# Merging the first unit's rows earlier, reads that do not hold scatters, plane copies on one engine, and a tile that starts elsewhere

## The chip, the cores and the metric

The kernel runs on one core of a Trainium2 chip, in one launch. The time is the device time of an execution in microseconds (us); the number that counts is the median of several. Engines are named as in the profile: PE is TensorE (PEld its weight loads), DVE is VectorE, ACT is ScalarE, POOL is GpSimd and SP is SyncE. Times of the trace count from the start of the span.

## The reference

Three stages follow one another, all in fp32:

```python
# 1. linear attention: batch 8, heads 8, sequence 576, head size 64
kv  = einsum('bhsd,bhse->bhde', k, v)
out = einsum('bhsd,bhde->bhse', q, kv)
x   = out / sqrt(mean(out*out, -1) + 1e-6) * g_norm      # -> 4608 tokens x 512
# 2. three first products, their maximum and relu, one second product (768 wide)
h = maximum(maximum(maximum(x @ w1, x @ w2), x @ w3), 0)
x = h @ w_out
# 3. 8 experts, the 2 best of each token by noisy logits
noisy = x @ w_gate + log1p(exp(x @ w_noise)) * noise
top2_w = exp(v - max(v)); top2_w /= sum(top2_w) + 1e-9   # v: the two best of noisy
for e in range(8):
    for k in range(2):
        out[mask] += top2_w[mask, k] * (maximum(x[mask] @ W1[e], 0) @ W2[e])   # W1 512x1024
```

## The kernel before

Each operand of a product is kept as a high part and a low part (the rest), both in a form that TensorE reads at full pace, and a product is three matmuls: high by high, weight's high by low, weight's low by high (the list `PASS`).

The program has two halves. **Chunks:** the 4608 tokens are done in nine chunks of 512. For each, `g1` makes the first products of stage 2 (L311), and `window(c)` the second product `g2` (L357) in four blocks of 128 tokens, each in two halves (`g2(c, i, 0, 3)`, `g2(c, i, 3, 6)`). Behind a block's second half its logits are copied out (L360) and its 512 values are cut in two planes of 16 bits and put into the tile RA (L364: half of the copies on VectorE, half on ScalarE). Routing (`route_a`, `route_b`) finds each token's two experts and its place among an expert's rows. `scatter(c, k)` writes the rows, with their weight and token number, to a table Xg in DRAM by four writes of GpSimd (L427), one for each block, for the best (k = 0) and the second expert (k = 1). The scatters of a chunk run in the next one. In chunk 8, at steps 11 to 17, the expert with most rows so far is picked (`spec_pick`) and the first work on it begins: its weights are loaded and split, and `load_rows(0)` reads 512 of its rows.

**Units:** the rows of the experts are done in 25 units of 512, 256 or 128 rows, that is four, two or one blocks. Units 0 to 3 have four, and then units of four alternate with smaller ones: units 4, 6 and 8 have one block, the even ones from 10 on two. Each has eight steps f. G1 (L1059; for one block L1073, rows by weights) makes 128 hidden columns; ScalarE and VectorE make their high and low parts behind relu (L1063, L1064). G2 (L1121) adds the second product, in four banks or fewer, and comes two steps later, by a queue (`fifo`); ScalarE scales its result (L1126) and GpSimd adds it to the output by row number (L1095). In a one-block unit, G1 makes 256 columns at every second f, as rows; two steps later `turn` has them transposed on TensorE (`hT1`, L1084), after ScalarE's relu (L1076), and ScalarE and VectorE make their parts (L1085, L1086).

The rows of a unit come in by `load_rows`: a transposing read on SyncE's queue (L755) of the planes, to RB (unit 0 and odd units) or RA, and a small read of weight and token number (`gt`, L756). `utrans(u, i)` then *merges* block i of unit u: two copies put the planes together as fp32 in one of two tiles mg (L784, the first on VectorE, the second on ScalarE), ScalarE writes the high part (L787), VectorE the low part (L788). The parts of even units go to one pair of tiles, those of odd units to B2 (high) and xlo (low). xlo holds 512 rows for all odd units, since these have four blocks.

Weights are loaded by SyncE as pairs (`load_pair`) and split by `splits`: ScalarE writes the high part (L292), VectorE the low part (L293), in a ring of 12 tiles W. The table `SPL` says how many splits follow each step of a unit.

Instructions are put on each engine's queue in the order in which the code emits them, and an engine takes them in that order. A framework adds the waits: an instruction waits for whatever wrote its inputs or still uses its output tile. For DRAM it can be told that accesses do not depend on each other (`declare_no_dep`, by group); the scatters are in such a group, "xg", and a read of rows gets by hand a dependency on every scatter issued so far (the list `written`). Before the change, a scatter issued after a read of rows waits for that read, since both touch Xg.

The order around the handover from chunks to units is written out: steps 11 to 17 of chunk 8 (`misc1`) with `load_rows(0)` at 12 and chunk 7's second scatter at 14, then `window(8)`. There, `nx` is false, and `trans(i)` means `utrans(0, i)`.

Of the kernel before, what the change touches and what calls it, by code (L numbers as in the profile page):

```python
# [12 lines left out]
U16 = mybir.dt.uint16  # L13
# [72 lines left out]
def body(tc, A, dbg=None):  # L86
    nc = tc.nc
    PE, ACT, DVE, POOL, SP = nc.tensor, nc.scalar, nc.vector, nc.gpsimd, nc.sync
# [8 lines left out]
    def st(name, shape, dt=F):  # L97
        return sb.tile(shape, dt, name=name)

    Xg = dr.tile([XR, 2 * XW], U16, name="Xg")  # L100
# [243 lines left out]
    rows = RA.rearrange("p (i w) -> p i w", i=4)  # L344
# [274 lines left out]
    for s in range(12):  # L619
# [6 lines left out]
        u = 2 + 0.1 * s if s > 1 else (0.2, 0.4)[s]  # L626
# [20 lines left out]
    for g in range(18):  # L647
# [4 lines left out]
        f = g // 3  # L652
# [62 lines left out]
    order = order + spare  # L715
    units = [{"S": 4, "4": 4, "2": 2, "1": 1}[k] for k, _ in order]
    regE, regS = {}, {}
    st("al1", [128, 16])
    spi = st("spi", [128, 3], I32)
    spf = st("spf", [128, 3])  # L720
    sp1 = st("sp1", [128, 8])
# [22 lines left out]
    gt = [st(f"gt{i}", [128, 4, 2]) for i in range(3)]  # L744
# [3 lines left out]
    def rplanes(u):  # L748
        n = 128 * units[u]
        return rbuf(u).bitcast(U16)[:, 0:8 * n].rearrange("p (k t) -> p k t", k=8)  # L750

    def load_rows(u):
        m = units[u]
        at = bass.ds(regS[u], 128 * m)
        for i in (SP.dma_start_transpose(out=rplanes(u), in_=Xg[at, 0:1024]),  # L755
                  SP.dma_start(gt[u % 3][:, 0:m, :].bitcast(U16),  # L756
                               Xg[at, 1024:1028].rearrange("(i p) w -> p i w", p=128))):
            for w in written:
                tc.add_manual_dep(i.ins, w.name, mybir.DependencyInfo(mybir.DependencyClass.Sync,
                                                                      mybir.DependencyReason.DATA), reason="rows")  # L760

    praw = {}

# [10 lines left out]

    xTu = [xT]

    def utrans(u, i):
        s = slice(i * 128, (i + 1) * 128)
        pl = rplanes(u)
        g = MG[mgn[0] % 2]  # L780
        mgn[0] += 1
        h = g.bitcast(U16).rearrange("p (k t z) -> p k t z", k=4, z=2)
        for q in range(2):
            (ACT.copy if q else DVE.tensor_copy)(h[:, :, :, q], pl[:, 4 * q:4 * q + 4, s])  # L784
        t = g.rearrange("p (k t) -> p k t", k=4)
        x = xTu[u % 2]
        ACT.activation(x[0][:, :, s], t, AF.Copy)  # L787
        DVE.tensor_tensor(x[1][:, :, s], t, x[0][:, :, s].bitcast(F), op=OP.subtract)  # L788
        if i == units[u] - 1:
            m = units[u]  # L790
            DVE.tensor_copy(wid[u % 3][:, 0:m], gt[u % 3][:, 0:m, 0])
            DVE.tensor_copy(idt[u % 3][:, 0:m], gt[u % 3][:, 0:m, 1])
# [71 lines left out]
    def window(c):  # L864
        nx = c + 1 < NCH

        def fill(i):
            if nx:
                if i == 0:
                    ao(c + 1, 1, [hbank(), hbank()])  # L870
                norm(c + 1, i + 2)

        def trans(i):
            xtrans(c + 1, i) if nx else utrans(0, i)

        if c == 0:
            for i in (2, 3):
                g2(0, i, 0, 3)
                trans(i)
                g2(0, i, 3, 6)  # L880
            xn_n[0] = 0
            return
        for i in range(4):
            g2(c, i, 0, 3)
            if i == 3:
                trans(2)
                trans(3)
            g2(c, i, 3, 6)
            if i == 1:
                trans(0)  # L890
                trans(1)
                fill(0)
                fill(1)
            if not nx:
                if i == 3:
                    load_rows(1)
                splits(1)

# [133 lines left out]
    fifo = []  # L1032
# [99 lines left out]
    def turn(s):  # L1132
        while late and late[0][0] <= s:
            hT1(*late.pop(0)[1:])

    def flush(s):
        while fifo and fifo[0][0] <= s:
            G2(*fifo.pop(0)[1:])

# [20 lines left out]

    pump = {0: 1, 2: 1, 3: 2, 4: 2, 5: 2, 6: 2, 8: 1, 9: 1}
    tg = table()
    SPL = {4: (2,) * 8, 2: (1,) * 8, 1: (0, 0, 0, 1, 0, 1, 1, 1)}

    def unit(u):
        mn = units[u + 1] if u + 1 < len(units) else 0
        for f in range(8):
            turn(step[0])
            G1(u, f)
            flush(step[0])  # L1170
            for _ in range(pump.get(step[0], 0)):
                next(tg, None)
            if u < 2:
                if f in (3, 5):
                    for i in range(2):
                        utrans(u + 1, f - 3 + i)
                if u == 1 and f == 7:
                    load_rows(3)
            splits(SPL[units[u]][f])
            if u > 1:  # L1180
                if f in (2, 4):
                    for i in range(f - 2, min(f, mn)):
                        utrans(u + 1, i)
                if f == (4 if mn == 4 else 2) and u + 2 < len(units):
                    regs_of(u + 2)
                    load_rows(u + 2)
                    loads()
            step[0] += 1
# [7 lines left out]
    for u in range(NUN):  # L1196
        unit(u)
# [52 lines left out]
```

## Time and profile before

| | |
|---|---|
| time, median of 3 runs | 1570.40 us (1568.75 to 1570.77) |
| time of the profiled execution | 1571.03 us |
| its span | 1569.3 us |
| PE busy | 1523.7 us, 97% |
| DVE busy | 789.9 us, 50% |
| ACT busy | 655.0 us, 42% |
| POOL busy | 219.2 us, 14% |
| G1 of the units (L1059), both operands | 464.8 us in 2112 matmuls |
| G2 of the units (L1121) | 441.5 us in 1800 matmuls |
| chunks' first products (L311) | 456.3 us in 2160 matmuls |

The span is the time between the first and the last instruction of the trace; the profiled execution took 1.7 us more than its span. A group's busy time counts the time in which at least one of its instructions ran. A wait is the time in which an engine stood idle before an instruction, put down to what ended it. Matmuls overlap in the pipeline, so the pace of TensorE is read from start to start, or from the chain of waits, which gives each piece only the time that no other covers.

### The profile page before, as it was taken

To read this page: it belongs to the slowest core of one execution; us is meant where nothing else is said; L and a number is where in the kernel's file an instruction comes from. 1 tells how busy PE (TensorE), PEld (TensorE's weight loads), DVE (VectorE), ACT (ScalarE), POOL (GpSimd) and SP (SyncE) were. 2 spreads that over 40 slices of the span, in tenths; PEclk is the share of its full clock that TensorE was granted. 3 is DMA by queue.
4 is the path that set the end of the run, shared out by engine and by line. 5 is a ranking of instruction groups with operands and counts; after the bars stand their busy time and mean duration, and the time that the engine had idled before them with its cause. 6 is when DMAs were issued, how large, how long until landed. Compare 5 with 4: busy or idle time off the path is not lost.

```text
span 1569.3 us, 23768 instructions
## 1 busy us (share of the span) xinstructions
PE 1523.7 (97%) x9564; PEld 1308.5 (83%) x9564; DVE 789.9 (50%) x1561; ACT 655.0 (42%) x1048; POOL 219.2 (14%) x326
## 2 busy tenths in 40 slices
PE   6999999999999999999999898999999999999997
PEld 5789989898989888887888787778888888888886
DVE  4985534353434343456454456365463554535543
ACT  3544323231313132243454446455464554645544
POOL 0000211102020202023211102101021010211102
PEclk8999999999999999999999999999999999999999
DMA  7322642031212101063676467666695766857654
GB/s 291 134 81 89 257 189 115 29 116 53 91 56 89 56 28 55 1 189 115 209 195 137 112 221 186 158 204 173 159 223 130 199 156 166 210 139 215 148 154 76
DMA packets 132292, 219.82 MB, mean 140 GB/s; under 512 B 96464, under 2 KB 96720, under 8 KB 114640
## 3 DMA queue, kind: packets, MB, share of 16 engines
q1 hardware_dynamic: 112320, 166.50, 33.4%
q0 software_dynamic: 19856, 51.73, 14.6%
q8 instruction: 77, 1.26, 0.3%
q14 instruction: 39, 0.32, 0.1%
HBM read 146.30 MB, written 51.72 MB: 126 GB/s over the span
## 4 chain that ended last, share of the span: by engine, by line
PE 51%; DVE 2%; ACT 2%; issue 0%; POOL 0%; POOLq 0%; ACTq 0%; DVEq 0%
PE bank L1059 25%; PE bank L1121 25%; ACT B L787 1%; PE bank L1073 1%; DVE G L930 0%; ACT W L292 0%; DVE xlo L788 0%; DVE mg L784 0%; DVE W L293 0%; POOL out L1095 0%; PE bank L1084 0%; ACT mg L784 0%; ACT xn L1076 0%; DVE B L1064 0%; DVE h L1086 0%
## 5 line engine op out<-in xcount | busy, mean ns | idle before, releaser
L311 PE MATMUL bank<-B,W 128*128 128x512 f32 (+1 forms) x2160 | 456.3, 372 | 6.4 <-ACT W L482 4.0
L311 PEld LDWEIGHTS bank<-B,W 128*128 128x128 f32 x2160 | 378.0, 190 | 76.0 <-ACT W L482 4.8
L1121 PE MATMUL bank<-W,B 128*128 128x512 f32 x1728 | 421.8, 390 | 0.0
L1121 PEld LDWEIGHTS bank<-W,B 128*128 128x128 f32 x1728 | 320.2, 188 | 65.6
L1059 PE MATMUL bank<-B,W 128*128 128x512 f32 (+1 forms) x1728 | 358.9, 345 | 5.4 <-ACT B L787 5.4
L1059 PEld LDWEIGHTS bank<-B,W 128*128 128x128 f32 x1728 | 281.9, 190 | 51.7 <-ACT B L787 6.0
L293 DVE TENSOR_TENSOR W<-G,W 128x1024 fp32r<-128x1024 f32 x200 | 242.2, 1223 | 123.4 <-ACT W L292 122.6
L292 ACT ACTIVATE W<-G 128x1024 fp32r<-128x1024 f32 x200 | 207.8, 1054 | 54.2 <-PE bank L1121 40.3
L1064 DVE SCALAR_TENSOR_TENSOR B<-bank,B 128x512 fp32r<-128x512 f32 (+1 forms) x176 | 103.7, 591 | 220.7 <-ACT B L1063 220.7
L1063 ACT ACTIVATE B<-bank 128x512 fp32r<-128x512 f32 (+1 forms) x176 | 90.6, 517 | 282.0 <-PE bank L1059 281.8
L357 PE MATMUL bank<-W,B 128*128 128x256 f32 (+1 forms) x1296 | 163.9, 285 | 0.0
L357 PEld LDWEIGHTS bank<-W,B 128*128 128x128 f32 x1296 | 160.1, 188 | 1.1
L427 POOL DMA_INDIRECT Xg<-RA,si x72 | 71.0, 986 | 529.9 <-issue 346.3
L329 DVE TENSOR_TENSOR hm<-hm,bank 128x512 f32<-128x512 f32 (+1 forms) x106 | 69.5, 656 | 132.4 <-PE bank L311 125.6
L315 ACT ACTIVATE B<-hm 128x512 fp32r<-128x512 f32 (+1 forms) x53 | 32.2, 607 | 185.2 <-DVE hm L329 185.2
L1059 PE MATMUL bank<-xlo,W 128*128 128x512 f32 x384 | 105.9, 398 | 0.0
L1095 POOL DMA_INDIRECT out<-xn,idt x37 | 60.8, 1644 | 276.8 <-ACT xn L1126 269.8
L1059 PEld LDWEIGHTS bank<-xlo,W 128*128 128x128 f32 x384 | 72.6, 189 | 16.4
L787 ACT ACTIVATE B<-mg 128x512 fp32r<-128x512 f32 x76 | 48.0, 632 | 71.9 <-DVE mg L784 71.8
L1095 POOL DMA_INDIRECT out<-x2T,idt x19 | 30.2, 1589 | 268.5 <-ACT x2T L1126 266.1
L364 ACT COPY RA<-bank 128x256 uint16<-128x256 uint16 x72 | 25.7, 372 | 89.0 <-DVE RA L364 77.1
L788 DVE TENSOR_TENSOR xlo<-mg,B 128x512 fp32r<-128x512 f32 x49 | 34.0, 693 | 38.7 <-ACT B L787 38.7
(184 smaller groups left out, 1020.1 us busy)
## 6 DMA issues: line engine op xcount, KB each, us to landing
G<-mw SPq DMA_DIRECT2D x100, 1024.0 KB, 5.0
G<-w1s SPq DMA_DIRECT2D x12, 1024.0 KB, 5.1
out<-pad POOLq DMA_DIRECT2D x1, 9472.0 KB
kv<-kv SPq DMA_DIRECT2D x8, 1024.0 KB, 8.2
G<-kv SPq DMA_DIRECT2D x8, 1024.0 KB, 10.1
RB<-qT SPq DMA_DIRECT2D x8, 1024.0 KB, 5.0
G<-kvr SPq DMA_DIRECT2D x7, 256.0 KB, 10.2
Xg<-RA,si POOLq DMA_INDIRECT x72, 2.7
```

Source lines behind the costliest of these rows:

```text
L292: ACT.activation(w[:, 0:1024], src, AF.Copy)
L293: DVE.tensor_tensor(w[:, 1024:2048], src, w[:, 0:1024].bitcast(F), op=OP.subtract)
L311: PE.matmul(bank[:, 0:t1 - t0], w_in(g)[:, a, k, s], x[b][:, k, t0:t1], start=n == 0 and k == 0, stop=n == 2 and k == 3)
L329: DVE.tensor_tensor(hm, hm, bank, op=OP.max)
L357: PE.matmul(x2b[i][z][:, 0:hi - lo], h[:, a, s], w[:, b, lo:hi], start=f == 0 and n == 0, stop=f == 5 and n == 2)
L427: i = POOL.indirect_dma_start(out=Xg, out_offset=bass.IndirectOffsetOnAxis(ap=idx, axis=0), in_=src, in_offset=None)
L787: ACT.activation(x[0][:, :, s], t, AF.Copy)
L1059: PE.matmul(bank[:, 0:n], w[:, a, k, s], x[b][:, k, 0:n], start=z == 0, stop=z == 11)
L1063: ACT.activation(h[:, 0, 0:n], bank[:, 0:n], AF.Relu)
L1064: DVE.scalar_tensor_tensor(h[:, 1, 0:n], bank[:, 0:n], 0.0, h[:, 0, 0:n].bitcast(F), op0=OP.max, op1=OP.subtract)
L1095: d = POOL.indirect_dma_start(out=A["out"], out_offset=bass.IndirectOffsetOnAxis(ap=idt[u % 3][:, i:i + 1], axis=0), in_=y, in_offset=None ...
L1121: PE.matmul(obank[i], h[:, a, s], w[:, b, ff % 2, :], start=ff == 0 and n == 0, stop=ff == 7 and n == 2)
```

## The change

Six edits. (1) A tile of 16 values a partition, `al1`, becomes one of 8, so every tile that is allotted later starts 32 bytes lower: xlo from byte 215328 of a partition (32 past a multiple of 64) to 215296 (a multiple of 64), and the two mg the other way, the first from 209792 to 209760. (2) The reads of rows of units 0 and 1 join the group "xg", so that scatters issued after them do not wait for them. (3) `utrans` gets `tight`: in a one-block unit both plane copies are made by VectorE. (4) In `window(8)`, blocks 0 and 1 of unit 0 are merged behind block 0, blocks 2 and 3 and the read of unit 1's rows behind block 1; before, the first two came behind block 1, the others in the middle of block 3 and the read at its end. (5) The queue `fifo` is sorted by unit and step, and G1 stands before `turn`. (6) `SPL` of one-block units puts fewer splits in the steps before the last two.

```diff
@@ -715,7 +715,7 @@
     order = order + spare
     units = [{"S": 4, "4": 4, "2": 2, "1": 1}[k] for k, _ in order]
     regE, regS = {}, {}
-    st("al1", [128, 16])
+    st("al1", [128, 8])
     spi = st("spi", [128, 3], I32)
     spf = st("spf", [128, 3])
     sp1 = st("sp1", [128, 8])
@@ -752,12 +752,18 @@
     def load_rows(u):
         m = units[u]
         at = bass.ds(regS[u], 128 * m)
-        for i in (SP.dma_start_transpose(out=rplanes(u), in_=Xg[at, 0:1024]),
-                  SP.dma_start(gt[u % 3][:, 0:m, :].bitcast(U16),
-                               Xg[at, 1024:1028].rearrange("(i p) w -> p i w", p=128))):
+        ds = [SP.dma_start_transpose(out=rplanes(u), in_=Xg[at, 0:1024]),
+              SP.dma_start(gt[u % 3][:, 0:m, :].bitcast(U16),
+                           Xg[at, 1024:1028].rearrange("(i p) w -> p i w", p=128))]
+        for i in ds:
+            if u < 2:
+                tc.declare_no_dep(i.ins, group="xg", reason="rows of chunks that came before")
             for w in written:
                 tc.add_manual_dep(i.ins, w.name, mybir.DependencyInfo(mybir.DependencyClass.Sync,
                                                                       mybir.DependencyReason.DATA), reason="rows")
+        if u < 2:
+            for i in ds:
+                tc.add_to_no_dep_group("xg", i.ins)
 
     praw = {}
 
@@ -774,14 +780,14 @@
 
     xTu = [xT]
 
-    def utrans(u, i):
+    def utrans(u, i, tight=False):
         s = slice(i * 128, (i + 1) * 128)
         pl = rplanes(u)
         g = MG[mgn[0] % 2]
         mgn[0] += 1
         h = g.bitcast(U16).rearrange("p (k t z) -> p k t z", k=4, z=2)
         for q in range(2):
-            (ACT.copy if q else DVE.tensor_copy)(h[:, :, :, q], pl[:, 4 * q:4 * q + 4, s])
+            (ACT.copy if q and not tight else DVE.tensor_copy)(h[:, :, :, q], pl[:, 4 * q:4 * q + 4, s])
         t = g.rearrange("p (k t) -> p k t", k=4)
         x = xTu[u % 2]
         ACT.activation(x[0][:, :, s], t, AF.Copy)
@@ -882,17 +888,20 @@
             return
         for i in range(4):
             g2(c, i, 0, 3)
-            if i == 3:
+            if nx and i == 3:
                 trans(2)
                 trans(3)
             g2(c, i, 3, 6)
-            if i == 1:
+            if nx and i == 1:
                 trans(0)
                 trans(1)
                 fill(0)
                 fill(1)
             if not nx:
-                if i == 3:
+                if i < 2:
+                    trans(2 * i)
+                    trans(2 * i + 1)
+                if i == 1:
                     load_rows(1)
                 splits(1)
 
@@ -1134,6 +1143,7 @@
             hT1(*late.pop(0)[1:])
 
     def flush(s):
+        fifo.sort(key=lambda x: x[1:3])
         while fifo and fifo[0][0] <= s:
             G2(*fifo.pop(0)[1:])
 
@@ -1160,13 +1170,13 @@
 
     pump = {0: 1, 2: 1, 3: 2, 4: 2, 5: 2, 6: 2, 8: 1, 9: 1}
     tg = table()
-    SPL = {4: (2,) * 8, 2: (1,) * 8, 1: (0, 0, 0, 1, 0, 1, 1, 1)}
+    SPL = {4: (2,) * 8, 2: (1,) * 8, 1: (0, 0, 0, 0, 0, 0, 1, 1)}
 
     def unit(u):
         mn = units[u + 1] if u + 1 < len(units) else 0
         for f in range(8):
+            G1(u, f)
             turn(step[0])
-            G1(u, f)
             flush(step[0])
             for _ in range(pump.get(step[0], 0)):
                 next(tg, None)
@@ -1180,7 +1190,7 @@
             if u > 1:
                 if f in (2, 4):
                     for i in range(f - 2, min(f, mn)):
-                        utrans(u + 1, i)
+                        utrans(u + 1, i, units[u] == 1)
                 if f == (4 if mn == 4 else 2) and u + 2 < len(units):
                     regs_of(u + 2)
                     load_rows(u + 2)
```

Edit 4 on VectorE, in chunk 8's window from block 0's copies on. B_85 holds the parts of unit 0's rows, mg_280 and mg_281 are the merge buffers, W_75 and W_76 tiles of split weights. Before:

```order
L364 COPY RA<-bank_110 128x256
L364 COPY RA<-bank_111 128x256
L293 TENSOR_TENSOR W_75<-G_84,W_75 128x1024
L360 COPY lgs<-bank_109 128x16
L364 COPY RA<-bank_112 128x256
L364 COPY RA<-bank_109 128x256
L784 COPY mg_280<-RB 128x512
L788 TENSOR_TENSOR B_85<-mg_280,B_85 128x4x128
L784 COPY mg_281<-RB 128x512
L788 TENSOR_TENSOR B_85<-mg_281,B_85 128x4x128
L293 TENSOR_TENSOR W_76<-G_82,W_76 128x1024
```

After:

```order
L364 COPY RA<-bank_110 128x256
L364 COPY RA<-bank_111 128x256
L790 COPY mg_280<-RB 128x512
L794 TENSOR_TENSOR B_85<-mg_280,B_85 128x4x128
L790 COPY mg_281<-RB 128x512
L794 TENSOR_TENSOR B_85<-mg_281,B_85 128x4x128
L293 TENSOR_TENSOR W_75<-G_84,W_75 128x1024
L360 COPY lgs<-bank_109 128x16
L364 COPY RA<-bank_112 128x256
L364 COPY RA<-bank_109 128x256
L790 COPY mg_280<-RB 128x512
```

Four merges move ahead: two past the split of W_75, and two past the splits of W_76 and W_77 and block 2's copies (of the second two the first copy is the last row).

Edit 5 on TensorE, from the first transposes of unit 4 (one block) to G1 of unit 5 (four blocks). xn_93 is the row of hidden values, L1084 the transposes, L1073 its G1, L1059 that of unit 5. Before:

```order
L1084 MATMUL bank_107<-cst,xn_93 128x128 x2
L1073 MATMUL bank_108<-W_72,B_85 128x256 x12
L1084 MATMUL bank_105<-cst,xn_93 128x128 x2
L1073 MATMUL bank_106<-W_74,B_85 128x256 x12
L1121 MATMUL bank_110<-W_71,h_0_6243 128x512 x6
L1084 MATMUL bank_107<-cst,xn_93 128x128 x2
L1073 MATMUL bank_108<-W_76,B_85 128x256 x12
L1121 MATMUL bank_110<-W_73,h_1_6244 128x512 x6
L1084 MATMUL bank_105<-cst,xn_93 128x128 x2
L1059 MATMUL bank_106<-B_87,W_78 128x512 x4
```

After (lines shifted by 9, so that L1093 are the transposes, L1082 and L1068 the two G1):

```order
L1082 MATMUL bank_107<-W_72,B_85 128x256 x12
L1093 MATMUL bank_108<-cst,xn_93 128x128 x2
L1082 MATMUL bank_105<-W_74,B_85 128x256 x12
L1093 MATMUL bank_106<-cst,xn_93 128x128 x2
L1130 MATMUL bank_110<-W_71,h_0_6243 128x512 x6
L1082 MATMUL bank_107<-W_76,B_85 128x256 x12
L1093 MATMUL bank_108<-cst,xn_93 128x128 x2
L1130 MATMUL bank_110<-W_73,h_1_6244 128x512 x6
L1068 MATMUL bank_105<-B_87,W_78 128x512 x4
L1093 MATMUL bank_106<-cst,xn_93 128x128 x2
```

Each transpose moves behind the G1 that followed it, the last one behind the first G1 of unit 5 (of its twelve matmuls the first four are shown).

Edits 3 and 6 on ScalarE, in the same unit. L1076 is relu, L784 a plane copy, L787 the high part, L1085 the high part of the transposed row, L292 a split. Before:

```order
L1085 ACTIVATE h_0_6243<-bank_107 128x256
L1076 ACTIVATE xn_93<-bank_108 128x256
L784 COPY mg_281<-RB 128x512
L787 ACTIVATE B_87<-mg_281 128x4x128
L784 COPY mg_280<-RB 128x512
L787 ACTIVATE B_87<-mg_280 128x4x128
L292 ACTIVATE W_80<-G_84 128x1024
L1085 ACTIVATE h_1_6244<-bank_105 128x256
L1076 ACTIVATE xn_93<-bank_106 128x256
```

After (L1085 is relu here, L1094 the transposed row's high part, L793 the merge's):

```order
L1085 ACTIVATE xn_93<-bank_107 128x256
L1094 ACTIVATE h_0_6243<-bank_108 128x256
L793 ACTIVATE B_87<-mg_281 128x4x128
L793 ACTIVATE B_87<-mg_280 128x4x128
L1085 ACTIVATE xn_93<-bank_105 128x256
L1094 ACTIVATE h_1_6244<-bank_106 128x256
L793 ACTIVATE B_87<-mg_281 128x4x128
L793 ACTIVATE B_87<-mg_280 128x4x128
L1085 ACTIVATE xn_93<-bank_107 128x256
L1094 ACTIVATE h_0_6243<-bank_108 128x256
L292 ACTIVATE W_80<-G_84 128x1024
```

The plane copies are gone, and the split of W_80 moves from between the merges to behind all four.

## Rows read from the trace of the kernel before

**Rows 1.** The page: busy us (share of the span) and instructions.

```profile
PE 1523.7 (97%) x9564; PEld 1308.5 (83%) x9564; DVE 789.9 (50%) x1561; ACT 655.0 (42%) x1048; POOL 219.2 (14%) x326
```

**Rows 2.** Waits of TensorE, whole span: total us, times, longest.

```profile
PE bank L1084 <- ACT xn L1076: 12.2, 9, 2.2
PE bank L1059 <- ACT B L787: 5.4, 2, 5.2
```

**Rows 3.** Timeline, TensorE, chunks to units: start, us, instructions, [idle before <- releaser].

```profile
685.97 17.73 PE L357 MATMUL bank<-W,B 128*128 128x256 f32 x144
708.91 10.19 PE L1059 MATMUL bank<-B,W 128*128 128x512 f32 x36 [5.22 <-ACT B L787]
718.94 2.88 PE L1121 MATMUL bank<-W,B 128*128 128x512 f32 x12
721.67 0.19 PE L412 MATMUL bank<-Cb,onesb 128*128 128x40 bf16 x1
```

**Rows 4.** Stretch 700 to 720: length, busy us of engines, clock, DMA share.

```profile
700.00:720.00 20.00, 14.78 (x72) 12.52 (x71) 10.85 (x40) 10.18 (x18) 0.00 (x0) 0.83 0.26 53
```

**Rows 5.** Timelines of SyncE, VectorE and GpSimd around chunk 7's second scatter.

```profile
673.64 11.45 SPq L755 DMA_TRANSPOSE RB<-Xg  x1
679.89 0.17 DVE L435 COPY RA<-wt 128x4 f32<-128x4 f32 x1
689.25 1.40 POOL L427 DMA_INDIRECT Xg<-RA,si  x1 [18.29 <-DMA gt<-Xg]
```

**Rows 6.** Timelines of VectorE and ScalarE (last row), merges of unit 0.

```profile
692.44 0.76 DVE L364 COPY RA<-bank 128x256 uint16<-128x256 uint16 x2 [1.71 <-DMA Xg<-RA,si]
694.65 1.23 DVE L293 TENSOR_TENSOR W<-G,W 128x1024 fp32r<-128x1024 f32 x1 [1.45 <-ACT W L292]
696.53 0.46 DVE L784 COPY mg<-RB 128x512 uint16<-128x512 uint16 x1
708.89 0.69 DVE L788 TENSOR_TENSOR B<-mg,B 128x512 fp32r<-128x512 f32 x1 [0.76 <-ACT B L787]
708.23 0.63 ACT L787 ACTIVATE B<-mg 128x512 fp32r<-128x512 f32 x1 [0.53 <-DVE mg L784]
```

**Rows 7.** Chain of waits, units 2 and 3: start, us, pieces.

```profile
832.00 2.72 PE bank L1059 x12
834.72 2.72 PE bank L1121 x12
837.44 2.77 PE bank L1059 x12
840.21 2.73 PE bank L1121 x12
```

**Rows 8.** Groups by form, TensorE: count, busy us, mean ns.

```profile
L1059 PE MATMUL bank<-xlo,W 128*128 128x512 f32 x384 | 105.9, 398 | 0.0
```

**Rows 9.** Timeline, TensorE, one-block unit 4 into unit 5.

```profile
895.18 0.44 PE L1084 MATMUL bank<-cst,xn 128*128 128x128 f32 x2 [1.41 <-ACT xn L1076]
900.64 0.69 PE L1084 MATMUL bank<-cst,xn 128*128 128x128 f32 x2 [2.19 <-ACT xn L1076]
900.99 2.06 PE L1059 MATMUL bank<-B,W 128*128 128x512 f32 x4
```

**Rows 10.** Timelines of VectorE, GpSimd and ScalarE in unit 4.

```profile
889.77 0.77 DVE L784 COPY mg<-RB 128x512 uint16<-128x512 uint16 x1
891.10 1.57 POOL L1095 DMA_INDIRECT out<-xn,idt  x1 [0.27 <-issue]
895.02 0.77 ACT L784 COPY mg<-RB 128x512 uint16<-128x512 uint16 x1
```

**Rows 11.** Stretch 900 to 904, columns as in rows 4.

```profile
900.00:904.00 4.00, 3.35 (x10) 2.73 (x11) 3.92 (x5) 2.75 (x6) 0.00 (x0) 0.57 0.41 113
```

**Rows 12.** Timelines of TensorE and ScalarE, start of unit 9.

```profile
1038.24 5.61 PE L1121 MATMUL bank<-W,B 128*128 128x512 f32 x24
1038.88 0.68 ACT L1126 ACTIVATE xn<-bank,wid 128x512 f32<-128x512 f32 x1
```


## The prediction

> **What bounds the kernel now.** I read the page's busy shares first, then what TensorE waited for, then the timelines around those waits, and last the chain of waits for the pace of matmuls that wait for nothing. TensorE is busy for 1523.7 us [rows 1] of a span of 1569.3, so time can be gained only where it waits, where its clock is granted low, or where its matmuls run slower than others of their kind. The table of waits names two places that this change touches: 12.2 us in nine waits of the one-block units' transposes (L1084) for ScalarE's row of hidden values, and 5.4 us in which G1 (L1059) waits for ScalarE's high part of a unit's rows (L787), 5.2 of them at once [rows 2].
>
> The one of 5.2 is the handover from the chunks to the units. Its matmuls end the last product of chunk 8 at 703.70, and G1 of unit 0 starts at 708.91 [rows 3]. It is paid twice, since the granted clock over 700 to 720 is 0.83 [rows 4]: 0.17 of 20 us, doubled, is some 6.8 us at the lower level (1.2 GHz), part of it after the idle time. So the 36 matmuls of three G1 took from 708.91 to 718.94, 10.03 us.
>
> Why the rows were late is in the rows of the other engines. SyncE issued the transposing read of unit 0's rows from 673.64 on. The second scatter of chunk 7 had its last operand from VectorE at about 680.1, but GpSimd started it at 689.25, after an idle 18.29 us that the read of the same rows ended [rows 5]. Until it had read its planes, VectorE could not copy block 0 of chunk 8 into them (692.44, after 1.71 idle), so the split of W (694.65) and the first merge (696.53) queued behind that, and the last high and low parts of unit 0 came at 708.23 and 708.89 [rows 6].
>
> **The change part by part.** *Handover.* The reads of units 0 and 1 no longer hold the scatters. Nothing else in front of them on GpSimd's queue moves, so chunk 7's second scatter starts at about 680.2 instead of 689.25 and its planes are free some 3.2 us later (692.44 less 689.25 is what block 0's copies waited for), at 683.4. Block 0 of chunk 8 is through TensorE at 685.97 plus a quarter of 17.73, 690.4 [rows 3], so its copies now wait only for the product. Block 0's four plane copies end at about 691.4 on VectorE (0.76 for its two [rows 6]). The merges of rows 0 and 1 follow there, each 0.46 (copy), 0.63 (high part), 0.69 (low part) [rows 6] and semaphores, about 2.1 in all for one that is alone, 1.8 when the copies lie beside the other: they end at 695.7. The split of W (1.23) ends at 697.2, block 1's copies at 698.4, and the merges of rows 2 and 3 at 702.2. G1 wants them at 703.7, so the wait of 5.2 goes with 1.5 to spare, and with it the drop of the clock: 10.03 less 3 x 2.72 [rows 7] is 1.87. That is 7.1; I take 7.0. Next late: block 1's copies must free their banks for block 3, which starts at 685.97 + 3 x 4.43 = 699.3 (0.9 to spare), and routing of chunk 8, whose counts TensorE sums at L412. That stood at 721.67 in a row with matmuls on both sides [rows 3] and comes 7 us earlier, while block 3's copies and the chain behind them come only 4 to 5 earlier; I work out 0.2 to 1.0 us to spare. SyncE's read for unit 1 moves up from 708 to 702; nothing stands behind it there that could go sooner. Bounds: 0 (the wait moves whole to a copy or the routing) and 8.5.
>
> *The aligned low part.* The shorter tile shifts all later tiles by 32 bytes, so xlo, at 32 past a multiple of 64 bytes before, starts on such a multiple; the merge buffers go the other way. xlo is the moving operand of the middle four matmuls of a G1 in odd units of two and four blocks. Unit 2, whose low part lies in another tile, shows G1 of 12 matmuls in 2.72 us and G2 in 2.72; unit 3, with xlo, 2.77 and 2.73 [rows 7]. Neither unit waits and the clock is whole. There are 384 such matmuls [rows 8], so 96 groups: 96 x 0.05 = 4.8, and with the 0.01 of the G2 behind, 5.8. I take 5.3. Odd units differ from even ones in nothing else that TensorE reads: same weights' ring, same shapes, and the high parts of both start on a multiple of 64. But no row shows xlo at another place, so the bounds are 0 and 5.8. A cost of merge buffers at 32 bytes: VectorE wrote xlo there in 0.69, as it did the aligned low part of unit 0 (0.69 [rows 6]); I set it to nothing.
>
> *One-block units.* In each of the three that run (units 4, 6, 8) the four-block unit that follows is merged. Twelve copies of 0.77 leave ScalarE [rows 10] and go to VectorE at 0.46, where the low part of the same merge now stands behind two copies in a row. A merge that was two copies side by side, 0.63 and 0.69 becomes 2 x 0.46, 0.63, 0.69, in one line: 2.25 to 2.3 against the 1.82 at which merges followed one another. Four of them and GpSimd's row writes beside the first two (a copy took 0.77 there [rows 10]) bring the last high part to about 900.3. G1 of the next unit now stands ahead of the last transposes on TensorE and waits for that high part instead: it starts at about 900.35, where in the trace of before it started at 900.99, behind its transposes [rows 9]. Of the three waits of a unit, 1.41 and 2.19 [rows 9] and the 0.47 that they leave of a third of 12.2, the first in time (0.47) goes, the second stays at some 1.2 to 1.7, and the third becomes one of about 2.45 at G1. Gain 0.4 a unit, 1.2 in all, with 0 and 1.2 a unit as its ends. Against that stand the splits that move to the end of these units and beyond: 2.0 us more of ScalarE lies in front of the merges in the first steps of the next unit. In unit 9, which merges a two-block unit at its end, ScalarE read the last output bank of unit 8 from 1038.88 to 1039.56; TensorE writes it anew with the tenth matmul after 1038.24, at 1040.3 [rows 12]. That slack of 0.7 is less than 2.0, so 1.3 is lost there, up to 2.0. And the one wait of 2.45 is longer than any before: the clock fell after unit 4's waits alone (0.57 over 900 to 904 [rows 11]), so this can give 1.4 back or cost as much in two more units. Together I take +0.4, between -5 and +5.
>
> Sum: 1571.03 (the profiled execution: span and 1.7 around it) - 7.0 - 5.3 + 0.4 = 1559.1. The median of the runs shown lies 0.63 lower, so 1558.5.
>
> **The rivals.** *The low part's slowness is not its place.* Then 5.3 stays: 1563.8. For it: in unit 3's G1 the four matmuls behind those on xlo are slow too, though they read the aligned high part, and only one place was ever run. Against: unit 2 and every G1 of unit 0 lack it.
>
> *The one-block waits go away*, as two engines share the merges better: 12.2 and the 1.4 of clock, 1558.5 - 14.0 = 1544.5. For it: ScalarE is the releaser of all nine. Against: the chain of copies above, which no engine shortens.
>
> *The rows come too late all the same.* The second scatter's four writes now run beside the transposing read, which took 11.45 us to issue [rows 5]; if they push its landing out by more than the 2 to 4 us to spare, or if the copies of block 1 come late for block 3, the wait of 5.2 stays in another place: 1558.5 + 7.0 = 1565.5. Against: TensorE's table shows no other wait on row reads, and only their sum must fit.
>
> *Slower: copies and row writes shut each other out.* In one-block units VectorE now makes eight copies of planes in a row while GpSimd writes the rows of the unit before, four writes of 1.57 us [rows 10]. If a copy could not run beside a write at all, each unit's merges would come up to 4 x 1.57 = 6.3 us later, straight onto G1: 19 us in three units, 1577. It decides once it costs more than the 11.9 that the other parts gain, 4 us a unit. Against it, one copy of 0.77 instead of 0.46 is all that the rows show of before, 0.31 a copy. The Trainium skill (SBUF — State Buffer, section "Who interferes with whom") has such a rule: a copy in a two-port mode and GpSimd take a shared pair of ports whole, and whoever comes second blocks fully. By that rule the trace agrees only in part: the copy was lengthened, but by a fifth of a write.
>
> **How the numbers follow.** A difference under 0.2%, 3.1 us, can't be told from none here. My forecast has 0.65; the low part unchanged 0.13; the one-block waits gone 0.07; the rows late 0.10; the copies shut out 0.05. Faster by over 0.2% means under 1567.3: all but the last, and but a tail of the late rows joined with an unchanged low part (1570.8): 0.92. Within 0.2% 0.04, slower 0.04. The forecast's own range is 1555 to 1562; reaching to the first and third rival gives 1553 to 1566, which leaves out the one-block waits gone and the copies shut out.
>
> **What would show it.** Handover: no wait of G1 at L1068 (1059 before) above 0.5 after the last product of chunk 8, clock 1.00 there, and GpSimd's scatter at about 680. Low part: unit 3's G1 in 2.72, and the mean of 96 groups down by 0.05. One-block units: a wait of about 2.4 at G1 for L793 in each, and one of 1 to 2 at L1130 at the start of unit 9. Wrong would be a time above 1566 or under 1553, G1 still at 2.77, or a wait at L412 or in the product of chunk 8 that takes up what the handover gives.

## The result and the profile after

The kernel after took 1556.27 us (median of 4, 1555.68 to 1557.19) where the kernel before took 1569.95 (median of 4): a ratio of 0.9914, 95% interval 0.9897 to 0.9931, or 13.7 us. 1558.5 was forecast. The profiled execution has a span of 1554.0 us.

The table of waits of TensorE, whole span, as [rows 2] of before (total us, times, longest):

```profile
PE bank L1068 <- ACT B L793: 6.9, 4, 2.3
PE bank L1130 <- ACT xn L1135: 1.9, 1, 1.9
PE bank L1093 <- ACT xn L1085: 0.8, 3, 0.3
```

The nine waits of 12.2 at the transposes are down to 0.8, and the handover's 5.2 is gone; in their place stand three waits of 2.3 at G1 (their fourth is small), and one of 1.9 at G2. Around the handover (timeline of TensorE, then a window with the granted clock behind POOL's count, then POOL, VectorE and ScalarE), answering [rows 3 to 6]:

```profile
684.57 17.73 PE L357 MATMUL bank<-W,B 128*128 128x256 f32 x144
702.13 8.33 PE L1068 MATMUL bank<-B,W 128*128 128x512 f32 x36
710.30 2.88 PE L1130 MATMUL bank<-W,B 128*128 128x512 f32 x12
```

```profile
700.00:720.00 20.00, 20.00 (x100) 16.77 (x99) 14.44 (x61) 9.38 (x17) 2.93 (x5) 1.00 0.32 78
```

```profile
678.47 1.69 POOL L427 DMA_INDIRECT Xg<-RA,si  x1 [8.93 <-DVE RA L435]
689.24 0.75 DVE L364 COPY RA<-bank 128x256 uint16<-128x256 uint16 x2
689.91 0.46 DVE L790 COPY mg<-RB 128x512 uint16<-128x512 uint16 x1
700.23 0.69 DVE L794 TENSOR_TENSOR B<-mg,B 128x512 fp32r<-128x512 f32 x1 [0.76 <-ACT B L793]
699.56 0.63 ACT L793 ACTIVATE B<-mg 128x512 fp32r<-128x512 f32 x1 [0.51 <-DVE mg L790]
```

The product of chunk 8 ends and G1 follows without a gap; 36 matmuls take 8.2 us to the next row's start (before: 10.03), and the clock of the window is 1.00 (before: 0.83). GpSimd's scatter starts with its operand, block 0's copies (689.24) wait only for the product, and the last high part (699.56 and 0.63) is 1.9 us ahead of G1.

The low part, from the chain of waits in unit 3, where before had 2.77 and 2.73 [rows 7], and the group of its matmuls, 398 ns each before [rows 8]:

```profile
839.14 2.72 PE bank L1068 x12
841.86 2.72 PE bank L1130 x12
```

```profile
L1068 PE MATMUL bank<-xlo,W 128*128 128x512 f32 x384 | 103.2, 391 | 0.0
```

In unit 4, and the same in 6 and 8 (timelines of TensorE, then VectorE and GpSimd; answers to [rows 9, 10]):

```profile
885.05 0.44 PE L1093 MATMUL bank<-cst,xn 128*128 128x128 f32 x2 [0.24 <-ACT xn L1085]
889.30 1.21 PE L1068 MATMUL bank<-B,W 128*128 128x512 f32 x4 [2.26 <-ACT B L793]
```

```profile
881.18 0.79 DVE L790 COPY mg<-RB 128x512 uint16<-128x512 uint16 x2
883.27 0.79 DVE L790 COPY mg<-RB 128x512 uint16<-128x512 uint16 x2
877.64 1.56 POOL L1104 DMA_INDIRECT out<-hm,idt  x1 [32.03 <-ACT hm L1135]
881.38 1.65 POOL L1104 DMA_INDIRECT out<-xn,idt  x1 [0.27 <-issue]
883.34 1.79 POOL L1104 DMA_INDIRECT out<-xn,idt  x1 [0.27 <-issue]
```

The transposes wait 0.24, and G1 of unit 5 waits 2.26 for the last high part. Two copies in a row take 0.79, less than twice 0.46, so a merge follows the other after 2.1 us (881.18 to 883.27). And at unit 9, against [rows 12] (TensorE, then ScalarE; the last row is a window with its clock):

```profile
1027.57 5.30 PE L1130 MATMUL bank<-W,B 128*128 128x512 f32 x15 [1.88 <-ACT xn L1135]
1032.71 1.08 PE L1068 MATMUL bank<-B,W 128*128 128x512 f32 x4
```

```profile
1020.10 2.00 ACT L292 ACTIVATE W<-G 128x1024 fp32r<-128x1024 f32 x2
1022.00 0.77 ACT L790 COPY mg<-RA 128x512 uint16<-128x512 uint16 x1
1026.84 0.68 ACT L1135 ACTIVATE xn<-bank,wid 128x512 f32<-128x512 f32 x1
```

```profile
1027.00:1033.00 6.00, 5.43 (x17) 4.34 (x18) 3.28 (x6) 2.41 (x3) 1.60 (x2) 0.72 1.18 277
```

The split of 2.00 stands ahead of the merges, the scaling of unit 8's rows (1026.84) comes 1.9 us late, and then 15 matmuls take 5.1 us to the next start where 3.4 is their time at the pace of unit 3 (12 in 2.72): the granted clock is 0.72 over six us.

**Where the time went.** The starts of the same matmuls in the two traces, as differences after less before: -1.4 us up to the last product of chunk 8 (-1.5 arises in the first 85 us, which the change doesn't touch, so it is put down to the two executions); -5.4 at G1 of unit 0 and -1.9 more by its first G2 (handover, -7.2); -0.53 in each of twelve odd units (low part, -6.4); units 4 to 9 together +0.1 without their three parts of that; -0.3 at the end. Their sum is -15.3, the difference of the two spans.

### The profile page after: what moved, and what is told of

Read it like the earlier page. It is cut to its first block, busy times and chain, and to the rows that moved or that the text cites. A ratio compares the mean times of both kernels' runs of the same rounds, so it can differ in the third digit from the quotient of the medians.

```text
span 1554.0 us, 23767 instructions
## 1 busy us (share of the span) xinstructions
PE 1515.0 (97%) x9564; PEld 1306.2 (84%) x9564; DVE 792.4 (51%) x1573; ACT 646.0 (42%) x1036; POOL 221.4 (14%) x326
## 4 chain that ended last, share of the span: by engine, by line
PE 92%; DVE 3%; ACT 2%; DMA 1%; issue 1%; POOL 1%; SPq 0%; POOLq 0%; ACTq 0%
PE bank L311 28%; PE bank L1068 24%; PE bank L1130 24%; PE bank L357 10%; PE bank L192 1%; PE bank L214 1%; PE bank L273 1%; DVE mg L790 1%; ACT B L793 1%; DMA pad<-kvr 1%; PE bank L1082 1%; DMA G<-kv 0%; POOL Xg L427 0%; DVE xlo L794 0%; PE bank L501 0%
## 5 line engine op out<-in xcount | busy, mean ns | idle before, releaser
L1068 PE MATMUL bank<-B,W 128*128 128x512 f32 (+1 forms) x1728 | 355.0, 343 | 6.9 <-ACT B L793 6.9
L1068 PEld LDWEIGHTS bank<-B,W 128*128 128x128 f32 x1728 | 280.9, 190 | 51.1 <-ACT B L793 8.7
L293 DVE TENSOR_TENSOR W<-G,W 128x1024 fp32r<-128x1024 f32 x200 | 242.1, 1223 | 120.2 <-ACT W L292 119.6
L292 ACT ACTIVATE W<-G 128x1024 fp32r<-128x1024 f32 x200 | 207.6, 1055 | 53.3 <-PE bank L1130 39.8
L1073 DVE SCALAR_TENSOR_TENSOR B<-bank,B 128x512 fp32r<-128x512 f32 (+1 forms) x176 | 103.8, 592 | 207.1 <-ACT B L1072 206.6
L1068 PE MATMUL bank<-xlo,W 128*128 128x512 f32 x384 | 103.2, 391 | 0.0
L1068 PEld LDWEIGHTS bank<-xlo,W 128*128 128x128 f32 x384 | 72.3, 188 | 15.1
L793 ACT ACTIVATE B<-mg 128x512 fp32r<-128x512 f32 x76 | 48.0, 632 | 84.4 <-DVE mg L790 84.3
```

Of the source, the lines that this page charges most:

```text
L292: ACT.activation(w[:, 0:1024], src, AF.Copy)
L293: DVE.tensor_tensor(w[:, 1024:2048], src, w[:, 0:1024].bitcast(F), op=OP.subtract)
L1068: PE.matmul(bank[:, 0:n], w[:, a, k, s], x[b][:, k, 0:n], start=z == 0, stop=z == 11)
L1073: DVE.scalar_tensor_tensor(h[:, 1, 0:n], bank[:, 0:n], 0.0, h[:, 0, 0:n].bitcast(F), op0=OP.max, op1=OP.subtract)
```

## The experiments

They ran on three other chips. On these the kernel before took 1576.35 (first four runs), 1576.33 (next four, with a rerun of after) and 1580.82 (last four); each ratio is to the kernel before on the same chip. Each of the twelve traces has 5.6 to 8.7 us more than the first pair between the first matmuls of chunk 1 and of chunk 4, the one of the kernel before with edit 1 alone too (7.0), and the kernel before itself is 6.4 to 10.9 slower there, so this belongs to those chips and not to the change. A second difference, in ScalarE, is told with the rerun of after. Stretches are therefore compared from the starts of the same matmuls.

**The low part's place, 32 and 16 bytes off.** In the kernel after, the tile alone:

```diff
-sb2.tile([128, 2048], FR, name="xlo")
+sb2.tile([128, 2056], FR, name="xlo")[:, 8:2056]     # 32 bytes; 16: 2052 and 4:2052
```

> The kernel after, with the tile of the low part alone put back to 32 bytes past a multiple of 64; nothing else moves. My theory (the place of the moving operand sets the pace): G1 of odd units back to 2.77 us, G2 behind it to 2.73, so 12 odd units lose 0.53 us each and the time is 6.4 us above the kernel after, about 1562.7. Rival (what sped up G1 is another tile that the shorter one moved, such as the merge buffers): the time of the kernel after, 1556.3, and G1 at 2.72.

> As the run before, but 16 bytes past a multiple of 64. If any start off a multiple of 64 bytes costs one more piece of each row read, the loss is the same as at 32, 6.4 us (1562.7). If the cost grows with the distance, or depends on 32 alone, it is another: half of it (3.2) or none (1556.3).

Ratios 0.9983 (0.9972 to 0.9993) and 0.9973 (0.9963 to 0.9983); the rerun of after had 0.9950 on its chip. The chain of waits in unit 3, at 32 bytes and then at 16:

```profile
862.82 2.77 PE bank L1068 x12
865.60 2.73 PE bank L1130 x12
```

```profile
863.76 2.75 PE bank L1068 x12
866.51 2.73 PE bank L1130 x12
```

Of what the odd units read, only this tile's place differs (the two tiles h1 allotted behind it move as well, but only one-block units read them), and G1 and the G2 behind it are back at 2.77 and 2.73. Unit 3 is longer than in after by 0.53, and so is every odd unit from 11 on. At 16 bytes it is 0.37 a unit: not the same as at 32, and not half. The rival with the other tiles falls; by what rule 16 bytes cost less than 32 stays open.

**Edit 1 alone.**

```diff
 # kernel before
-    st("al1", [128, 16])
+    st("al1", [128, 8])
```

> The kernel before with the shorter tile alone (edit 1). Theory: the low part's 12 x 0.53 = 6.4 us come off whatever else is done, 1569.95 - 6.4 = 1563.6, and handover and one-block units stay as before (G1 of unit 0 waits 5.2, L1084 waits 12.2 in all). Rival (the gain exists only with the other edits): 1570.

1571.60 against 1576.35, ratio 0.9965 (0.9953 to 0.9977): 4.7 us between the medians, 5.5 by the ratio, with bounds of 3.6 and 7.4. Each odd unit from 11 on is 0.53 shorter than in the trace of before, and the waits are those of before:

```profile
PE bank L1084 <- ACT xn L1076: 12.3, 9, 2.2
PE bank L1059 <- ACT B L787: 4.6, 2, 4.4
```

The gain of the low part needs no other edit.

**One-block units as before.** In the kernel after: `utrans(u + 1, i)` without `tight`, `turn` ahead of G1, `fifo` not sorted, and the old row of `SPL`.

> The kernel after without edits 3, 5 and 6: plane copies on two engines, transposes ahead of G1, the old table of splits. Theory (edits 3, 5 and 6 give 1.6 us in each one-block unit and lose them again at unit 9 and by the clock): 1556 to 1557, the same as after within 1 us; waits of L1093 of 12 us in all are back and the wait of L1130 in unit 9 is gone. Rival (the one-block units gave part of the 13.7 us): 1559 or more.

Ratio 0.9934 (0.9917 to 0.9950), 10.6 us under before; the rerun of after on the next chip had 7.4 under, and the intervals overlap (0.9935 to 0.9966). From the first G1 of unit 4 to that of unit 10 it took 184.4 us, after 182.9 in its first trace and 184.4 in its second. So edits 3, 5 and 6 together gain nothing that the runs show; what each does alone is told under "Edit 3 alone undone". The nine waits at the transposes are back, and none is left at unit 9's G2:

```profile
PE bank L1093 <- ACT xn L1085: 12.3, 9, 2.2
```

**After again, edit 2 undone, edit 4 undone.**

```diff
 # no_dep_off: load_rows
-            if u < 2:
-                tc.declare_no_dep(i.ins, group="xg", ...)
...
-                tc.add_to_no_dep_group("xg", i.ins)
 # old_window: window(8)
-                if i < 2:
-                    trans(2 * i)
-                    trans(2 * i + 1)
-                if i == 1:
+                if i == 3:
                     load_rows(1)
```

(with edit 4 undone, `trans` stands again where it stood before)

> The kernel after itself, beside the runs that undo a part of it, since the chip of the last runs gave the kernel before 6.4 us more than the first (1576.35 against 1569.95) and gave three kernels with edit 4 a wait of 1.6 to 3.2 at the first G1 of unit 1 that the first trace of after doesn't have. If that wait belongs to the chip or its run, after has it here too where before takes about 1576, and the ratio is 0.993; where before takes about 1570 it has none, and the ratio is 0.991. If it belongs to edits of the experiments, after never has it.

> The kernel after without edit 2: scatters wait for the reads of units 0 and 1 again, the merges stay behind blocks 0 and 1. As the prediction has it (the scatter's wait is why the rows were late) the handover wait of G1 comes back in good part, 3 to 7 us with the clock. My theory now, from the trace of before: the scatter held only block 0's copies, by 1.7 us; merges move by 1.7, the high parts still come in time, and TensorE waits about 1 us in the last product of chunk 8 for block 1's copies: 1 us above after.

> The kernel after without edit 4: merges of unit 0 where they were before, scatters not held. If the scatter's wait was the cause, the handover stays repaired: no wait, same time as after. My theory (the place of the merges behind block 2's copies and two splits is the cause): G1 of unit 0 waits 4.3 to 5.2 us and the clock takes 1.9 again, 6 to 7 us above after.

Ratios 0.9950 (0.9935 to 0.9966), 0.9964 (0.9954 to 0.9975) and 0.9968 (0.9956 to 0.9981). TensorE at the handover, without edit 2, then without edit 4; in both the row of the last product and that of G1:

```profile
691.50 18.35 PE L357 MATMUL bank<-W,B 128*128 128x256 f32 x144
709.69 8.34 PE L1063 MATMUL bank<-B,W 128*128 128x512 f32 x36
```

```profile
689.87 17.73 PE L357 MATMUL bank<-W,B 128*128 128x256 f32 x144
711.98 10.50 PE L1065 MATMUL bank<-B,W 128*128 128x512 f32 x36 [4.39 <-ACT B L793]
```

Without edit 2, with GpSimd's scatter again 18 us idle, the product lasts 0.6 longer (18.35 and no gap), routing's matmul at L412 comes 0.4 later still, and G1 of unit 0 has no wait. Without edit 4, with the scatter on time, the wait of 4.39 and the low clock are back. So the place of the merges made the wait, 6.7 us with the clock; that the scatter was late cost 1.0. The medians show only 2.5 us between the rerun of after and the run without edit 4, because the rerun loses 4.9 us at unit 1, which the other does not.

The rerun has what the first trace of after lacks, a wait of 3.2 at unit 1. ScalarE and GpSimd in this trace, and TensorE's first G1 of unit 1:

```profile
734.10 0.58 ACT L1072 ACTIVATE B<-bank 128x512 fp32r<-128x512 f32 x1
742.76 0.60 ACT L1072 ACTIVATE B<-bank 128x512 fp32r<-128x512 f32 x1 [8.08 <-PE bank L1068]
```

```profile
740.12 1.08 POOL L427 DMA_INDIRECT Xg<-pad,si  x1 [0.22 <-issue]
```

```profile
752.81 1.20 PE L1068 MATMUL bank<-B,W 128*128 128x512 f32 x4 [3.22 <-ACT B L793]
```

ScalarE's row says that it waited for TensorE until 742.76, but the matmuls of that G1 were over some 6.8 us earlier (where ScalarE is free, the other relus of unit 0 come within 0.1 us of the end of their G1), and it makes its relu 1.6 us behind the end of the last of GpSimd's eight writes of padding rows. In the first trace of after the same relu stood at 726.97, in the middle of these writes and on time. All eleven traces of the other chips with the writes in their old place have it late: by 2.3 to 2.4 us where the handover still waits (edit 1 alone, edit 4 undone), by 5.3 to 7.0 in the others, and it comes between 1.5 us ahead of the end of the last write and 1.7 behind it. An earlier handover moves the relu ahead more than the end of what holds it, and so 3.1 us are given back at G1 of unit 1 in the rerun, and 1.8 behind it, where the granted clock is 0.72 over 752 to 758.

**The splits of unit 9, twice.** In the kernel after, once the splits of such a unit's step behind its merges, once none at step 2:

```diff
 # split_behind
-            splits(SPL[units[u]][f])
...                                   # behind utrans, where u > 1, four blocks, and mn == 2
+                    splits(SPL[units[u]][f])
 # skip_split
+            splits(0 if u > 1 and mn == 2 and f == 2 else SPL[units[u]][f])
```

> The kernel after with one thing moved: in units of four blocks that merge a unit of two, each step's splits stand behind that step's merges instead of ahead. Theory (unit 9's wait of 1.9 at L1130 comes from the split of 2.0 us that ScalarE and VectorE do just ahead of the merges, and the clock doubles it): that wait goes, 15 matmuls behind it take 3.4 instead of 5.3, and the time is 3.5 to 3.8 under after. Rival (the wait is only passed on, to the weights split later): 0 to 1 under after, and a wait at L1068 or L1130 for L292 or L293 in units 9 to 23.

> The kernel after, with no split at step 2 of four-block units that merge a unit of two (the splits come in the steps behind). Theory (splits of 2.0 us ahead of the merges, and ahead of unit 8's last scaling, make the wait of 1.88 at L1130 in unit 9; moving them behind the merges left 1.16 since they still stood ahead of that scaling): the wait is gone, 15 matmuls behind it take 3.4 us, unit 9 is 1.9 shorter, and up to 1.9 more where the clock had dropped: 2 to 4 us under after. Rival (the splits are missed later): a wait for L292 or L293 in units 9 to 23 takes it back.

Ratios 0.9939 (0.9916 to 0.9963) and 0.9916 (0.9900 to 0.9933; the chip of the last four). TensorE in unit 9, first and second:

```profile
1038.54 3.71 PE L1130 MATMUL bank<-W,B 128*128 128x512 f32 x15 [1.16 <-ACT xn L1135]
```

```profile
1039.97 5.60 PE L1130 MATMUL bank<-W,B 128*128 128x512 f32 x24
1045.41 1.07 PE L1068 MATMUL bank<-B,W 128*128 128x512 f32 x4
```

Behind the merges the split still stands ahead of the scaling, and 1.16 is left. So neither expectation came out: the wait did not go, and the waits for L292 or L293 that the rival named did not come; unit 9 is 0.8 shorter than in the first trace of after and 2.3 than in its rerun. Without a split at step 2 the 24 matmuls run through in 5.4 us, and again no wait for L292 or L293 comes later. From unit 9 to unit 10 it takes 2.24 less than in the first trace of after, and 3.77 less than in its rerun.

**Merges two steps earlier.** The run before, and:

```diff
-                if f in (2, 4):
-                    for i in range(f - 2, min(f, mn)):
+                f0 = f + 2 if units[u] == 1 else f
+                if f0 in (2, 4):
+                    for i in range(f0 - 2, min(f0, mn)):
```

> The run before, and the four merges in one-block units begin at steps 0 and 2 instead of 2 and 4. Theory (the wait of 2.26 at L1068 in each is the end of the line of copies and merges on VectorE, which starts too late): the wait is gone in three units, 6.8 us less, and with it the drops of the clock behind it; 7 to 10 us under after in all with the split. Rival (row writes of GpSimd or ScalarE's scalings of the unit before hold the earlier merges): 1 to 3 us of waits stay in each unit, now at L1082 or L1093.

1556.22 against 1580.82, ratio 0.9855 (0.9839 to 0.9872); against the run before on the same chip 10.6 us less. G1 of unit 5, and the waits at L1068, whose one left is that of unit 1:

```profile
897.72 1.86 PE L1130 MATMUL bank<-W,h 128*128 128x512 f32 x6
899.42 1.08 PE L1068 MATMUL bank<-B,W 128*128 128x512 f32 x4
```

```profile
PE bank L1068 <- ACT B L793: 2.1, 1, 2.1
```

By its ratio it is the fastest of all the runs and beats both kernels: its interval lies wholly under those of after. From unit 4 to unit 10 its trace is 11.9 us shorter than that of the run before; 6.8 of them are the three waits, and the rest is some 1.7 in each of units 5, 7 and 9, where the clock had fallen behind them. Windows of ten us around G1 of unit 5, without and with this edit (clock 0.83 and 1.00):

```profile
900.00:910.00 10.00, 7.73 (x28) 5.86 (x27) 6.76 (x12) 6.28 (x10) 0.00 (x0) 0.83 0.34 100
```

```profile
897.00:907.00 10.00, 9.72 (x45) 7.58 (x44) 7.70 (x12) 6.99 (x13) 1.46 (x2) 1.00 0.72 160
```

**Edit 3 alone undone.** `utrans(u + 1, i)` without `tight`.

> The kernel after without edit 3 alone: plane copies of one-block units on VectorE and ScalarE, G1 ahead of the transposes, the new table of splits. The prediction's reasoning (two copies in one line make a merge longer: 2.1 measured, against 1.82 with two engines): the wait of 2.26 at L1068 shrinks by about 4 x 0.27 = 1.1 in each of three units, 3 us under after. Rival (ScalarE's copies of 0.77 hold its hidden rows, which is what L1093 waited for before): waits of 0.5 to 2 at L1093 come back, and the time is 0 to 5 us above after.

Ratio 0.9900 (0.9881 to 0.9919), where the run without the split at step 2, which is 2.2 to 3.8 us shorter than after, had 0.9916. In unit 5 (timeline of TensorE):

```profile
902.93 1.20 PE L1068 MATMUL bank<-B,W 128*128 128x512 f32 x4 [1.73 <-ACT B L793]
```

The wait shrank by 0.5, and G1 of units 5, 7 and 9 starts 1.1 earlier in each. No wait at L1093 is back. So edit 3 by itself costs 1.1 us a unit; what removed the waits at the transposes was the order on TensorE and the later splits (edits 5 and 6). The clock adds to it: in ten us around G1 of units 5, 7 and 9 it is 1.00 here, and from unit 4 to unit 10 this trace takes 176.3 us, after 182.9 and 184.4, and the run without edits 3, 5 and 6 had 184.4. Edits 5 and 6 without edit 3 thus gain some 8 us in this stretch, and edit 3 gives 6.6 to 8.1 of them back: that is why the three together gain nothing.

**Padding rows later.**

```diff
         scatter(c, 0)
-        pads()
...
                 scatter(c, 1)
+                pads()
```

> The kernel after, with GpSimd's eight writes of padding rows moved from behind the scatter of the best experts of chunk 8 to behind the scatter of the second ones, 13 us later. On the chips of the last two jobs ScalarE made the relu of unit 0's sixth G1 6.8 us after TensorE had it, which cost 3.1 us at unit 1. If the writes that run at that time hold ScalarE, the relu is on time here (within 0.3 us of its G1) and unit 1 starts without that wait. If not (ScalarE is held by something that goes by its own program), it is late as before by 5 to 7 us. On a chip where after has no such gap the run tells nothing of this. The next reads of rows wait for the later writes: 0 to 4 us at unit 2.

Ratio 0.9968 (0.9956 to 0.9981). ScalarE at the sixth relu of unit 0, where the writes now run, and at a later split; GpSimd's last write; and TensorE in unit 1:

```profile
737.17 0.60 ACT L1072 ACTIVATE B<-bank 128x512 fp32r<-128x512 f32 x1 [1.32 <-PE bank L1068]
754.17 0.60 ACT L1072 ACTIVATE B<-bank 128x512 fp32r<-128x512 f32 x1 [2.13 <-PE bank L1068]
762.35 0.60 ACT L1072 ACTIVATE B<-bank 128x512 fp32r<-128x512 f32 x1 [7.58 <-PE bank L1130]
778.12 2.00 ACT L292 ACTIVATE W<-G 128x1024 fp32r<-128x1024 f32 x2 [12.86 <-DMA G<-mw]
```

```profile
759.81 0.97 POOL L427 DMA_INDIRECT Xg<-pad,si  x1 [0.22 <-issue]
```

```profile
780.66 1.22 PE L1130 MATMUL bank<-W,B 128*128 128x512 f32 x2 [4.54 <-ACT B L1072]
```

The sixth relu is on time (737.17) and unit 1 starts 2.9 us earlier than in the rerun of after, counted from the start of unit 0. A gap moved with the writes: the next late relu is at 762.35, 2.5 us behind its G1 and again 1.6 us behind the last write, while the one before it, in the middle of the writes (754.17), is on time. TensorE does not wait for it. The wait of 4.5 at unit 1's G2 is another thing: that G2 needs a relu that stands on ScalarE behind a split, and the split waited for its weights until 778.12. These were issued at 768.3, as in the rerun of after (768.5), but took 9.8 us to land instead of 7.1, and TensorE came to this G2 3.3 us earlier; why they landed later stays open. So on these chips ScalarE is held for a part of the time in which GpSimd makes these writes, as far as one run with the writes moved can show. Why it stands, why its end lies now ahead of the last write and now behind it, and why the first chip's traces have no such gap, stays open: no row of a queue or an engine shows it, and the instruction queues of the trace have no packet between 732 and 763 in the rerun.

## Why the prediction was right, and where not

*Handover.* Forecast -7.0, measured -7.2, with the clock at 1.00 as said, and routing reached TensorE at L412 with 0.3 us to spare (0.2 to 1.0 forecast). The step that failed is its reason, "Why the rows were late": it put the queue of W's split and the merges down to the scatter. The scatter held block 0's copies alone, worth 1.0 (0.6 in the product, 0.4 at L412); the merges were late because they stood behind block 1's copies and, two of them, behind two splits and block 2's copies. Undoing edit 4 with the scatter free brought the wait back. "Nothing stands behind it there" and "bounds: 0" overlooked a thing that lies further on: on three chips ScalarE is held during GpSimd's padding writes, and in the rerun 3.1 us went back there and 1.8 to the clock. That the chip of the first pair has no such gap is luck: on the rerun's chip 1.8 of 6.7 were left.

*Low part.* The mechanism was right, and the size was low: 0.53 a unit, 6.4 in all, against 5.3 taken and an upper bound of 5.8. The term failed by rounding: it came from 0.05 and 0.01 of a piece, where the whole unit gives 0.53 over 16 pieces; the pair of starts of a unit would have given it from the trace of before. I had leaned under the row's own 5.8 for no reason that a row gave. (The odd units all have four blocks, not two and four; the count of 384 matmuls holds.)

*One-block units.* Forecast +0.4, measured +0.1, by luck: the terms each missed and cancelled. A merge in one line takes 2.1 and not 2.25 to 2.3, and GpSimd's writes did not lengthen the copies, so G1 waits 2.26 where 2.45 was said, the other waits came to 0.2 and not 1.2 to 1.7, and the waits of a unit shrink by 1.6 instead of 0.4. Unit 9's wait came at the place and size forecast (1.9; 1.3 to 2.0), and the clock took 1.7 more behind it (5.1 less 3.4), and 1.7 in unit 7 (43.15 us long, 41.45 with the merges two steps earlier), while before's loss in unit 5 was won. The sizes that failed are the merge's length and the wait left at the transposes. The prediction put one price on edits 3, 5 and 6 together; the run with two engines shows that edit 3 cost what the other two gained.

*The rivals.* That the low part's place didn't matter fell with the tile moved back. That the one-block waits vanish did not come by this change; merging two steps earlier brought it. The rows were not late. Copies and row writes do not shut each other out to the loss of the copies: where a write began behind them they took 0.79 for two, as the later two pairs of unit 4 did with no write beside them, and the writes took 1.65 and 1.79 instead of 1.56. The Trainium skill's rule (SBUF — State Buffer, "Who interferes with whom") has whoever comes second wait for the whole of the other, if the copy is in a two-port mode; the trace does not tell the mode, and shows the write that came second lengthened by at most 0.23, a third of a pair of copies.

*The forecast's number* came out 2.2 us high, from 1.1 on the low part, 0.3 on the one-block units, 0.2 on the handover, and the rest from the executions themselves. It holds for the chip of the first pair: where ScalarE is held the same change brought 7.4.

## What to carry over

The operand that TensorE streams here ran fastest from a multiple of 64 bytes (16 and 32 past one were slower; no other place was tried). Such a cost is found by comparing the pace of two groups of equal shape that wait for nothing, and proved by moving one tile. A late operand can be late by its place in an engine's queue and not by the wait that is seen first, so count what stands ahead of it once that wait is gone; the wait that was removed here was worth a seventh of the order that was changed with it (1.0 and 6.7 us). When waits only move, ask where the chain of the late engine starts: beginning the merges two steps earlier gained 10.6 us where moving the copies to one engine lost 1.1 a unit and more by the clock.

## What the runs showed of the hardware

The start of a moving operand of 2048 bytes a partition sets the pace of matmuls: a unit with 32 matmuls on it took 0.53 us more at 32 bytes past a multiple of 64 and 0.37 more at 16 past, against a start on a multiple. Two copies of planes in a row on VectorE took 0.79, one 0.46. After waits of one length (2.26 at G1) the granted clock fell in unit 7 and not in units 5 and 9 of the first trace of after; after waits of 1.73, with the copies on two engines, it fell in none of the three. While GpSimd made eight indirect writes in a row, an instruction of ScalarE stood for up to 7.0 us on three chips, and not on the first.
